# A limit of eight exponential tiles in flight in place of twelve, a ring of 13 tiles in place of 21, and spectral differences in tiles of their own

## The chip, the cores and the metric

The kernel runs on one core of one Trainium2 chip. The metric is the device time of one execution in microseconds (us); smaller is better. Engines: PE is TensorE (matrix products), ACT is ScalarE, DVE is VectorE, POOL is GpSimd, and SP starts most transfers. One launch computes the whole reference.

## What is computed

`x` is 2048 rows of 512 numbers. Two kinds of layers alternate, twice each: a filter in the two-dimensional spectrum, and attention with 32 query heads of 16 numbers that share one key head and one value head.

```python
def _A_ref(x, w_r, w_i):
    X = rfft2(x.astype(float32), axes=(-2, -1))
    y = irfft2(X * (w_r + 1j * w_i), s=(S, D), axes=(-2, -1)).astype(bfloat16)
    return y

def _B_ref(x, wq, wk, wv, wo):
    q = (x @ wq).reshape(B, S, 32, 16).transpose(0, 2, 1, 3)
    k, v = x @ wk, x @ wv
    scores = einsum("bhqd,bkd->bhqk", q, k) * 16 ** -0.5
    o = einsum("bhqk,bkd->bhqd", softmax(scores), v)
    return o.transpose(0, 2, 1, 3).reshape(B, S, 512) @ wo

x = x + _A_ref(_layernorm(x), w_r, w_i)
x = x + _B_ref(_layernorm(x), wq, wk, wv, wo)
x = x + _A_ref(_layernorm(x), w_r, w_i)
x = x + _B_ref(_layernorm(x), wq, wk, wv, wo)
```

Here `B` is 1, `S` is 2048, `D` is 512.

## The kernel before, in words

**A planner writes the order.** When the program is built, class `Plan` keeps a clock for each engine and, step by step, takes the piece of work that can start first by its own cost table (`MM` 220 ns for a round of products on PE, `ACT_EXP` 908 ns, `DVE_P1` 600 ns). Each choice emits the real instruction, through class `Emit`. Each engine then runs its instructions in the order in which they were emitted, and waits only on semaphores. What the planner counts, such as buffers in use, exists while the program is built; on the chip only the order and the waits are left.

**A pair of layers.** One `Layer` object is a spectral layer and the attention layer behind it; there are two. The spectral layer is a transform along each row on PE, a four-point step across the rows on DVE (`radix_g`), the middle of the transform on PE (`mid`), the product with the filter (`filt`), a step of sums and differences on DVE (`radix_d`, L58, "spectral differences" below), the inverse on PE (`inv`, L1211), a four-point step (`radix_v`, L66 to L76) and the last product back to rows. Then follow the normalization, K, V and the queries. Each layer's four groups `t` of rows deliver a part of K and V each, and attention begins with the first of them.

**Attention.** There are 32 blocks of four heads and 512 queries; a block has 16 chunks of 128 keys. A unit is one head, 512 queries, 128 keys. PE makes the scores of a unit with keys in one strip of 32 rows (`scores`, L1331). ACT takes units in pairs from the double buffers `sa` and writes the exponentials into a tile `e` (`exp`, L1336). DVE takes single units from the buffers `b`, with a first pass in whole numbers (`p1`, L1343) and two further phases that POOL mostly does (`phase`, L1347). PE then adds up V products, four heads at a time in four column strips (`pv`, L1353): one for each unit of ACT, three for each unit of DVE. Which engine takes which unit is decided by the planner as it goes (`peek`, `take`).

**The limit on tiles in flight.** `live["ACT"]` goes up when a pair's scores are emitted (`do_scores`) and down when the last V product that reads its tile is emitted (`do_pv`). `usable("ACT")` is false while `live["ACT"] >= bufs["ACT"]`, and then no scores for ACT may be emitted. `round` picks the heads of the next V round; it takes fewer than four heads only where the block has no more, where nothing else can go on, or where `full` holds, that is where `live` has reached `bufs` for ACT or for DVE:

```python
full = self.force or any(self.live[k] >= self.bufs[k] for k in ("ACT", "DVE"))
return sel if len(sel) == 4 or self.made(b0) or full else None
```

`bufs["ACT"]` is 8 (`E_BUFS`) from the middle of a layer's spectral part (`add_middle`) and 12 (`E_LATE`) from the moment its fourth V is complete (`v_got` in `add_back`).

**The ring of tiles.** `Emit.e2` holds 21 tiles of 1024 two-byte numbers in each partition. `t2` takes the one that has been free longest, `free2` puts one back at the end of the list. Who takes tiles: the exponentials, turned rows for the row transform (`tr_evac`, `turned`), `V` and the sums of `radix_v`, and the two halves of each spectral difference (`L.Dz`, two tiles for each of four groups `u`, each given back after its fourth reader in `inv`). Other tiles, of 2048 numbers, come from the pool `work` with tags (`t4`).

Of the kernel before, what the change touches and what calls it, by code (L numbers as in the profile page):

```python
# [8 lines left out]
ACT = mybir.ActivationFunctionType  # L9
# [43 lines left out]
    return tabs  # L53


def radix2(nc, o, x, piece):

    nc.vector.tensor_tensor(out=o, in0=x[:, 0:2, :], in1=x[:, 2:4, :], op=ALU.subtract if piece else ALU.add)  # L58


def radix4(nc, sd, x, half, o, piece):
# [53 lines left out]
class Plan:  # L115
# [12 lines left out]
    PORT = True  # L128
    POOL_LAG = 2600.0
    E_BUFS = 8  # L130
    E_LATE = 12
    T_BUFS = 4
    WIN = 3413.0
    WARM = 3500.0
# [552 lines left out]
class Layer:  # L687
# [83 lines left out]

    def add_middle(self):
        p, em = self.plan, self.em
        p.bufs["ACT"] = p.E_BUFS
        self.mid, self.fil = [], []
        for u in range(4):
            evs, two = [], u in self.two

            if two:
                outs = [((0, 2), (0, 1), 0), ((1, 3), (0, 1), 2)]  # L780
            else:
                outs = [((0, 1, 2, 3), (0, 1), 0), ((0, 1, 2, 3), (2, 3), 2)]
            if u % 2:
                outs = [(ts, (k,), o + i) for ts, ks, o in outs for i, k in enumerate(ks)]
            for ts, ks, o in outs:
                base, prev = None, []
                for t in ts:
                    deps, take = [self.g_done[t]] + prev, None
                    if not prev:
                        deps = deps + (self.gate if len(ks) == 2 else self.mm1_done[T - 1])  # L790
                        take = "sa" if len(ks) == 2 else "b"
                    k = p.add("PE", 434.0 * len(ks), deps, lambda k, u=u, ks=ks, t=t, ts=ts, base=base:
                              em.mid(self, u, ks, t, ts, (base or k).slot), take=take, order=10 + u)
                    base, prev = base or k, [k]
                evs.append(p.add("ACT", 909.0 if len(ks) == 2 else 482.0, prev, lambda k, u=u, o=o, n=len(ks), base=base:
                                 em.mid_evac(self, u, o, n, base.slot), give=(base,), order=10 + u))
            if two:
                evs = [self.pieces((600.0, 600.0), evs, lambda i, u=u: em.turn(self, u, i), 10 + u)]
            if u == 3 and not two:
                a = p.add("DVE", 1733.0, evs[:2], lambda k, u=u: em.filt(self, u, 0, 2), order=10 + u, port=True)  # L800
                mu = p.add("DVE", 1733.0, evs[2:] + [a], lambda k, u=u: em.filt(self, u, 2, 4), order=10 + u, port=True)
            else:
                mu = p.add("DVE", 3466.0, evs, lambda k, u=u: em.filt(self, u, 0, 4), order=10 + u, port=True)
            self.fil.append(mu)
            self.mid.append(self.pieces((600.0, 600.0), [mu], lambda i, u=u: em.radix_d(self, u, i), 26 if self.direct else 10 + u))
# [5 lines left out]
    def add_back(self):  # L811
        p, em, at = self.plan, self.em, self.at
        left = [T]
        for t in range(T):
# [53 lines left out]
            def v_got(k, t=t):  # L868
                at.v_ready[t] = k.end + p.LAT[k.eng]
                left[0] -= 1  # L870
                if left[0] == 0:
                    p.bufs["ACT"] = p.E_LATE
                if left[0] == self.EARLY:
                    at.dve_on = True
                    at.dve_from = k.end - 2000.0
# [61 lines left out]
class Emit:  # L937


    def __init__(self, ctx, tc, ins, out):  # L940
        nc = self.nc = tc.nc
        A_x, self.w_r, self.w_i, B_wq, B_wk, B_wv, B_wo = ins
        mk = lambda nm, b=1, **kw: ctx.enter_context(tc.tile_pool(name=nm, bufs=b, **kw))
        const = mk("const")
        psum = mk("psum", space=bass.MemoryType.PSUM)
        self.pool = mk("work")
        self.sa = [psum.tile([P, 2, 512], F32, name=f"sa{i}") for i in range(2)]
        self.b = [psum.tile([P, 512], F32, name=f"b{i}") for i in range(Plan.NB)]
        nc.scalar.preload_act_table_set("natural_log_exp_and_others")
        self.x = const.tile([P, R, T, 512], BF, name="x_sb")  # L950
        self.xv = A_x.flatten_outer_dims().rearrange("(r p t) d -> p r t d", r=R, p=P, t=T)
        ht = host_tables()
        self.dram = {k: nc.inline_tensor(v, name=f"const_{k}").ap() for k, v in ht.items()}
        tabs = {name: const.tile(list(ht[name].shape), BF, name=f"tab_{name}") for name in ("ident", "PH", "PS")}
        self.ident, self.PH, self.PS = tabs["ident"], tabs["PH"], tabs["PS"]
        nc.scalar.dma_start(out=self.ident, in_=self.dram["ident"])
        nc.scalar.dma_start(out=self.PH, in_=self.dram["PH"])
        self.way = mk("way", 2, space=bass.MemoryType.DRAM)
        self.wq = const.tile([P, NC, D], BF, name="wq")
        self.wk = const.tile([P, NC, DH], BF, name="wk")  # L960
        self.wk8 = const.tile([P, NC, P], BF, name="wk8")
        self.part = const.tile([P, 2], F32, name="part")
        self.wv = const.tile([P, NC, DH], BF, name="wv")
        self.tc = tc
        self.e2 = [const.tile([P, 1024], BF, name=f"e2_{i}") for i in range(21)]
        self.idle, self.home, self.writer = list(range(21)), {}, {}
        self.WO = const.tile([P, 4, D], BF, name="WO")
        self.junk = const.tile([P, 512], BF, name="junk")
        self.eps = const.tile([P, 1], F32, name="eps")
        self.zero = const.tile([P, 512], BF, name="zero")  # L970
        self.KA = const.tile([P, S], BF, name="KA")
        self.KB = const.tile([P, S], BF, name="KB")
        self.warm = const.tile([P, 2, 16], U16, name="warm")
        nc.vector.memset(self.zero, 0.0)
        nc.vector.memset(self.eps, EPS)
        nc.gpsimd.memset(self.warm, 0)
        self.key = const.tile([P, 1], F32, name="key")
        self.pw = phase_weights()
        self.VS = [const.tile([P, NT, 32], BF, name=f"vs{i}") for i in range(1 + K_PH)]
        for i, v in enumerate(self.VS):  # L980
            nc.gpsimd.memset(v, 1.0 if i == 0 else self.pw[i - 1])
        nc.gpsimd.int64_add(self.warm[:, 1].bitcast(U64), self.warm[:, 0].bitcast(U64), 0)
        half = (np.arange(P)[:, None] // DH % 2 == np.arange(2)).astype(np.float32)
        self.w_dma = [(self.PS, self.dram["PS"]), (self.wq, B_wq.rearrange("(c p) j -> p c j", p=P)),
                      (self.wk, B_wk.rearrange("(c p) j -> p c j", p=P)), (self.wv, B_wv.rearrange("(c p) j -> p c j", p=P)),
                      (self.part, nc.inline_tensor(half, name="const_part").ap()),
                      (self.WO, B_wo.rearrange("(g p) c -> p g c", p=P))]
        self.out_v = out.flatten_outer_dims().rearrange("(r p t) d -> p r t d", r=R, p=P, t=T)
# [178 lines left out]
    def turn(self, L, u, piece):  # L1167
        if piece == 0:
            L.sd_of[("x", u)] = self.t4([4, 512])
        radix2(self.nc, L.sd_of[("x", u)][:, 2 * piece:2 * piece + 2, :], L.X[u], piece)  # L1170
        if piece:
            L.X[u] = L.sd_of.pop(("x", u))

# [14 lines left out]

    def radix_d(self, L, u, piece):
        if piece == 0:  # L1190
            L.Dz[u] = [[self.t2([2, 512]), 4] for _ in range(2)]
            for z, _ in L.Dz[u]:
                self.writer.pop(self.home[id(z)][0], None)
        radix2(self.nc, L.Dz[u][piece][0], L.X[u], piece)

    def load_it(self, L, t):
        L.IT[t] = self.t4([4, 640], tag="it", bufs=2)
# [2 lines left out]
    def inv(self, L, t, b, j, slot, ks):  # L1200
        for v in range(T):
            if v <= t + 1 and v not in L.IT:
                self.load_it(L, v)
        ps = self.ps(slot).rearrange("p (u x) -> p u x", u=2)
        for k in ks:
            u = 2 * j + k
            for a in range(2):
                for i in range(2):
                    w = 128 * (3 - (t * a + i) % 4)
                    z = L.Dz[u][t % 2][0][:, a, 256 * i + 128 * b:256 * i + 128 * b + 128]  # L1210
                    self.nc.tensor.matmul(ps[:, k, :], lhsT=z, rhs=L.IT[t][:, u, w:w + 256], start=(a == 0 and i == 0),  # L1211
                                          stop=(a == 1 and i == 1), skip_group_check=True)
            d = L.Dz[u][t % 2]
            d[1] -= 1
            if d[1] == 0:
                self.free2(d[0])

    def inv0(self, L, b, j, slot, k):

# [255 lines left out]
```

## Time and profile before

| what | value |
| --- | --- |
| median of three runs | 1340.67 us (1340.6 to 1340.95) |
| the profiled execution | 1340.67 us |
| its span, first to last instruction | 1338.9 us |
| granted TensorE clock | 1.000 |
| attention of layer 1, first to last exponential | 73.9 to 674.3 us, 624 pairs on ACT, 800 units on DVE |
| attention of layer 2 | 736.1 to 1326.4 us, 619 pairs on ACT, 810 units on DVE |
| the wait of ACT for the scores of an exponential, longest two | 2.6 us, 2.2 us |

How to read what follows. The page gives each engine's busy time and its share of the span, then the span in 40 equal slices with the busy share in tenths; the row PEclk is the clock granted to TensorE in tenths. A stretch row begins with its limits in us and its length, then busy us and, in brackets, the number of instructions. A row of the timeline has start, duration, engine, line, operation and `out<-in`. A piece of the chain of waits has its start, its length, the engine, the tile, the line and the number of instructions. Several matmuls with the same start lie in different strips and run side by side; ends of matmuls are modelled, so their starts are read.

### The profile page before, as it was taken

To read this page: it belongs to the slowest core of one execution; us is meant where nothing else is said; L and a number is where in the kernel's file an instruction comes from. 1 tells how busy PE (TensorE), PEld (TensorE's weight loads), DVE (VectorE), ACT (ScalarE), POOL (GpSimd) and SP (SyncE) were. 2 spreads that over 40 slices of the span, in tenths; PEclk is the share of its full clock that TensorE was granted. 3 is DMA by queue.
4 is the path that set the end of the run, shared out by engine and by line. 5 is a ranking of instruction groups with operands and counts; after the bars stand their busy time and mean duration, and the time that the engine had idled before them with its cause. 6 is when DMAs were issued, how large, how long until landed. Compare 5 with 4: busy or idle time off the path is not lost.

```text
span 1338.9 us, 31412 instructions
## 1 busy us (share of the span) xinstructions
PE 1298.0 (97%) x12913; PEld 438.9 (33%) x12982; DVE 1281.7 (96%) x2297; ACT 1231.0 (92%) x1401; POOL 834.9 (62%) x819
## 2 busy tenths in 40 slices
PE   9999999999999999999999999999999999999998
PEld 4642223322232332222246422233222222232222
DVE  6998999999999999999979999999999999999998
ACT  6478999999999999999944899999999999999996
POOL 0004777766776678667720067787777767777775
PEclk9999999999999999999999999999999999999999
DMA  9100000010001000000051000000000000000000
GB/s 292 41 1 1 2 1 2 2 33 1 1 2 33 1 2 2 17 17 1 2 166 40 1 2 1 2 1 5 13 2 1 4 15 1 1 2 17 1 2 17
DMA packets 29040, 25.15 MB, mean 19 GB/s; under 512 B 8672, under 2 KB 27616, under 8 KB 28896
## 3 DMA queue, kind: packets, MB, share of 16 engines
q1 hardware_dynamic: 28608, 22.58, 5.6%
q8 instruction: 101, 1.65, 0.5%
q10 hardware_dynamic: 288, 0.56, 0.1%
q14 instruction: 43, 0.35, 0.1%
HBM read 17.89 MB, written 3.67 MB: 16 GB/s over the span
## 4 chain that ended last, share of the span: by engine, by line
ACT 48%; PE 30%; DVE 17%; issue 2%; DMA 1%; SPq 1%; POOL 0%; DVEq 0%; POOLq 0%
PE sa_64 L1331 3%; PE b_66 L1353 3%; PE b_69 L1353 3%; PE b_67 L1353 3%; ACT e_5_89 L1336 2%; ACT e_3_87 L1336 2%; ACT e_4_88 L1336 2%; ACT e_16_100 L1336 2%; PE sa_65 L1331 2%; ACT e_10_94 L1336 2%; ACT e_11_95 L1336 2%; ACT e_15_99 L1336 2%; ACT e_8_92 L1336 2%; ACT e_14_98 L1336 2%; ACT e_9_93 L1336 2%; ACT e_20_104 L1336 2%
## 5 line engine op out<-in xcount | busy, mean ns | idle before, releaser
L1331 PEld LDWEIGHTS <-KB 32*128 32x128 bf16 x2048 | 89.0, 91 | 229.0 <-issue 221.5
L1331 PEld LDWEIGHTS <-KA 32*128 32x128 bf16 x2048 | 83.4, 91 | 229.0 <-issue 219.4
L1353 PEld LDWEIGHTS <-vs_116 128*32 128x32 bf16 x2486 | 102.1, 94 | 97.6 <-issue 91.4
L1353 PEld LDWEIGHTS <-vs_117 128*32 128x32 bf16 x1610 | 97.1, 94 | 69.8 <-issue 68.1
L1353 PEld LDWEIGHTS <-vs_118 128*32 128x32 bf16 x1610 | 73.1, 94 | 75.7 <-issue 70.8
L1353 PEld LDWEIGHTS <-vs_119 128*32 128x32 bf16 x1610 | 71.9, 94 | 72.5 <-issue 67.9
L1347 POOL INT64_ADD w_1388<-w_1387 x1 | 1.0, 1039 | 110.7 <-DVE w_1387 L1343 110.7
L1347 POOL INT64_ADD w_10887<-w_10886 x1 | 1.0, 1037 | 98.5 <-DVE w_10886 L1343 98.5
L1040 DVE BATCH_NORM_STATS2 st<-x_sb 128x6 f32<-128x512 bf16 x52 | 35.4, 680 | 4.2 <-DMA x_sb<-in_A_x_dram 3.7
L1336 ACT ACTIVATE e_6_90<-sa_65 128x1024 bf16<-128x1024 f32 x32 | 35.4, 1107 | 1.3 <-PE sa_64 L1331 1.0
L1336 ACT ACTIVATE e_7_91<-sa_64 128x1024 bf16<-128x1024 f32 x33 | 36.2, 1097 | 0.3 <-PE sa_64 L1331 0.3
L1336 ACT ACTIVATE e_12_96<-sa_65 128x1024 bf16<-128x1024 f32 x32 | 35.5, 1110 | 0.9 <-PE b_68 L1331 0.8
L1336 ACT ACTIVATE e_14_98<-sa_65 128x1024 bf16<-128x1024 f32 x31 | 34.7, 1119 | 1.5 <-PE sa_64 L1331 1.4
L1336 ACT ACTIVATE e_13_97<-sa_65 128x1024 bf16<-128x1024 f32 x32 | 35.9, 1122 | 0.0
L1336 ACT ACTIVATE e_20_104<-sa_64 128x1024 bf16<-128x1024 f32 x32 | 35.9, 1121 | 0.0
L1336 ACT ACTIVATE e_8_92<-sa_65 128x1024 bf16<-128x1024 f32 x31 | 34.6, 1116 | 1.1 <-PE b_69 L1331 0.8
L1336 ACT ACTIVATE e_2_86<-sa_64 128x1024 bf16<-128x1024 f32 x32 | 35.3, 1103 | 0.0
L1336 ACT ACTIVATE e_17_101<-sa_65 128x1024 bf16<-128x1024 f32 x28 | 31.8, 1135 | 3.6 <-PE sa_64 L1331 3.6
L1336 ACT ACTIVATE e_4_88<-sa_64 128x1024 bf16<-128x1024 f32 x31 | 35.0, 1129 | 0.0
L1336 ACT ACTIVATE e_0_84<-sa_65 128x1024 bf16<-128x1024 f32 x30 | 33.5, 1117 | 1.3 <-PE sa_64 L1331 1.0
L1336 ACT ACTIVATE e_16_100<-sa_64 128x1024 bf16<-128x1024 f32 x31 | 34.6, 1118 | 0.0
L1336 ACT ACTIVATE e_17_101<-sa_64 128x1024 bf16<-128x1024 f32 x31 | 34.5, 1113 | 0.0
(4068 smaller groups left out, 6441.8 us busy)
## 6 DMA issues: line engine op xcount, KB each, us to landing
it<-const_IT SPq DMA_DIRECT2D x8, 640.0 KB, 6.3
x_sb<-in_A_x_dram SPq DMA_DIRECT2D x4, 512.0 KB, 6.9
out_dram<-x_sb SPq DMA_DIRECT2D x16, 128.0 KB, 1.8
way<-x_sb SPq DMA_DIRECT2D x6, 256.0 KB, 2.1
tab_PH<-const_PH ACTq DMA_DIRECT2D x1, 512.0 KB, 5.0
w_131<-const_FT SPq DMA_DIRECT2D x1, 512.0 KB, 8.8
w_136<-const_FT SPq DMA_DIRECT2D x1, 512.0 KB, 8.4
tab_PS<-const_PS SPq DMA_DIRECT2D x1, 512.0 KB, 7.8
```

The lines of the kernel that those rows point to most:

```text
L1040: self.nc.vector.bn_stats(st, self.ps(slot) if slot else self.x[:, x[1], x[0], :])
L1331: self.nc.tensor.matmul(o, lhsT=KX[rs, kc * P:(kc + 1) * P], rhs=at.QT[qb][rs, g, :], start=True, stop=True, skip_group_check=True)
L1336: self.wrote("ACT", e, self.nc.scalar.activation(out=e, in_=self.ps(slot), func=ACT.Exp, scale=SCALE))
L1347: self.nc.gpsimd.int64_add(t[p][:, 0:n].bitcast(U64), t[0][:, 0:n].bitcast(U64), DELTA[p] * FOUR)
L1353: self.nc.tensor.matmul(self.ps(slot)[32 * h:32 * h + 32, :], lhsT=V[:, kc, :], rhs=rhs, start=first, stop=last, skip_group_check=True)
```

## The change

The diff does three things.

1. The limit on ACT's pairs in flight stays at `E_BUFS`, 8; `E_LATE` is gone, in both layers.
2. The ring `e2` has 13 tiles in place of 21.
3. The spectral differences leave the ring. Each group `u` gets one tile of 2048 numbers under a tag of its own, `xd`, with four buffers; both halves lie in it. `inv` reads the same rows from there and gives nothing back. `radix2` takes the whole tile and the number of the half, and `turn` is written for that.

The diff comes with the words "Score heads of ScalarE's pairs and VectorE's tiles are chosen so that they lie in different 32-row strips of TensorE"; `peek`, which chooses the heads, is not in it.

```diff
-def radix2(nc, o, x, piece):
-
-    nc.vector.tensor_tensor(out=o, in0=x[:, 0:2, :], in1=x[:, 2:4, :], op=ALU.subtract if piece else ALU.add)
+def radix2(nc, sd, x, piece):
+
+    nc.vector.tensor_tensor(out=sd[:, 2 * piece:2 * piece + 2, :], in0=x[:, 0:2, :], in1=x[:, 2:4, :],
+                            op=ALU.subtract if piece else ALU.add)
...
     E_BUFS = 8
-    E_LATE = 12
...
     def add_middle(self):
         p, em = self.plan, self.em
-        p.bufs["ACT"] = p.E_BUFS
...
                 left[0] -= 1
-                if left[0] == 0:
-                    p.bufs["ACT"] = p.E_LATE
...
-        self.e2 = [const.tile([P, 1024], BF, name=f"e2_{i}") for i in range(21)]
-        self.idle, self.home, self.writer = list(range(21)), {}, {}
+        self.e2 = [const.tile([P, 1024], BF, name=f"e2_{i}") for i in range(13)]
+        self.idle, self.home, self.writer = list(range(13)), {}, {}
...
         if piece == 0:
             L.sd_of[("x", u)] = self.t4([4, 512])
-        radix2(self.nc, L.sd_of[("x", u)][:, 2 * piece:2 * piece + 2, :], L.X[u], piece)
+        radix2(self.nc, L.sd_of[("x", u)], L.X[u], piece)
...
         if piece == 0:
-            L.Dz[u] = [[self.t2([2, 512]), 4] for _ in range(2)]
-            for z, _ in L.Dz[u]:
-                self.writer.pop(self.home[id(z)][0], None)
-        radix2(self.nc, L.Dz[u][piece][0], L.X[u], piece)
+            L.Dz[u] = self.t4([4, 512], tag="xd", bufs=4)
+        radix2(self.nc, L.Dz[u], L.X[u], piece)
...
-                    z = L.Dz[u][t % 2][0][:, a, 256 * i + 128 * b:256 * i + 128 * b + 128]
+                    z = L.Dz[u][:, 2 * (t % 2) + a, 256 * i + 128 * b:256 * i + 128 * b + 128]
...
-            d = L.Dz[u][t % 2]
-            d[1] -= 1
-            if d[1] == 0:
-                self.free2(d[0])
```

## The prediction, made before the result was known

> **What bounds the kernel.** I read the busy row and the slices of the page first, then stretches of one engine at a time, then the chain of waits inside the worst stretch, then single tiles in the order of time.
>
> ```profile
> PE 1298.0 (97%) x12913; PEld 438.9 (33%) x12982; DVE 1281.7 (96%) x2297; ACT 1231.0 (92%) x1401; POOL 834.9 (62%) x819
> ...
> DVE  6998999999999999999979999999999999999998
> ACT  6478999999999999999944899999999999999996
> ...
> PEclk9999999999999999999999999999999999999999
> ```
>
> ScalarE (ACT) and VectorE (DVE) are full in slices 4 to 19 and 24 to 39: the two attention phases. The spectral phases lie in slices 1 to 3 and 20 to 23, where ACT has room. The clock is full throughout and is left out of what follows. What attention is worth per us comes from the stretches, taken for the exponentials (L1336, two units of 512 keys-by-queries each) and for VectorE's first pass (L1343, one unit each):
>
> ```profile
> core 0: us, ACT busy (x), PEclk, DMA share, GB/s
> 130.00:280.00 150.00, 149.80 (x164) 1.00 0.02 5
> 785.00:940.00 155.00, 154.84 (x170) 1.00 0.01 3
> ...
> 307.40:320.50 13.10, 12.08 (x13) 1.00 0.01 1
> 1074.40:1088.30 13.90, 13.68 (x16) 1.00 0.09 29
> ...
> core 0: us, DVE busy (x), PEclk, DMA share, GB/s
> 130.00:280.00 150.00, 133.90 (x220) 1.00 0.02 5
> 785.00:940.00 155.00, 141.13 (x232) 1.00 0.01 3
> ...
> 307.40:320.50 13.10, 7.09 (x13) 1.00 0.01 1
> 1074.40:1088.30 13.90, 8.81 (x16) 1.00 0.09 29
> ```
>
> Undisturbed attention does (2 x 164 + 220) / 150 = 3.65 units per us, and (2 x 170 + 232) / 155 = 3.69. I use 3.67. In the two short stretches it does (26 + 13) / 13.1 = 2.98 and (32 + 16) / 13.9 = 3.45: TensorE (PE) also has projection or query work there, and VectorE gets too few scores (13 first passes in 13.1 us, where 232 in 155 us would give 20). ACT keeps nearly its pace of 0.91 us a pair. So PE's order decides in the bursts, and ACT with DVE outside them.
>
> **Where the change can bite.** The limit on ACT's pairs in flight goes from 12 to 8 after the last V of a layer. A pair is in flight from its two sa matmuls on L1331 until the second of its two matmuls on L1353. Both stand in PE's own order, so the planner's count can be read off the trace: plus one at each pair's scores, minus one at the second reader.
>
> ```profile
> 400.26 1.24 ACT L1336 ACTIVATE e_18_102<-sa_64 128x1024 bf16<-128x1024 f32 x1
> ...
> 401.87 0.39 PE L1353 MATMUL b_67<-e_18_102,vs_116 128*32 128x512 bf16 x2
> ...
> 1076.76 1.18 ACT L1336 ACTIVATE e_19_103<-sa_65 128x1024 bf16<-128x1024 f32 x1
> ...
> 1087.08 0.39 PE L1353 MATMUL b_67<-e_19_103,vs_116 128*32 128x512 bf16 x2
> ```
>
> In plain attention a tile is read 1.6 us after its exponential began and the count is 2 to 4. In the burst the tile waits 10.3 us. Over the whole trace the count is above 8 for 31.0 us in seven places, with these peaks: 284 us (10), 307 to 320 (11), 574 (10), 942 (10), 1074 to 1093 (12), 1139 (9), 1227 (9). The sum of peaks less 8 is 2 + 3 + 2 + 2 + 4 + 1 + 1 = **15 pairs** that could no longer be put off. Pairs scored while the count stood above 8 number 42. Before 241.6 us the count does not reach 8 once the first V is complete, so until then PE's order should be that of before.
>
> **The limit, priced.** While the count stands at 8, PE may not score for ACT; `full` (in `round`) also lets it run a round of V products with fewer than four heads. It does V products, VectorE's scores or projections, then scores again. The pieces of the chain in the burst give the durations:
>
> ```profile
> 1079.30 0.32 PE sa_64 L1331 x2
> 1079.62 0.33 PE b_66 L1353 x4
> ...
> 1080.60 0.32 PE sa_65 L1331 x2
> 1080.93 0.55 PE b_66 L1353 x8
> ```
>
> Scoring a pair alone takes 0.32 us; a round of four V products takes 0.33, and a second round behind it 0.55 - 0.33 = 0.22. A pair needs half a round, 0.165 us. Putting off D pairs lets ACT run ahead by D half rounds. Without that, PE spends the same time on score and retirement together, so ACT loses D x 0.165 / (0.32 + 0.165) = 0.34 D pairs. For D = 15 that is 5.1 pairs, 10.2 units, and 10.2 / 3.67 = **2.8 us**. Ends: if every one of the 15 is lost to ACT, 30 / 3.67 = **8.2 us**. If ACT's other score buffer always covers the delay (it has about 0.91 - 0.32 = 0.6 us to hide one round) the loss is 0. I take 2.8, since both engines are full on either side of a burst and PE is nearly always busy within it. Queued behind a late pair on ACT are the flexible copies of queries and, in layer 2's front, the scalings on L1124; VectorE's radix steps wait for those.
>
> The Trainium skill, "TensorEngine Tiling (Array Packing)", section Key Properties, says that changing the tiling mode drains TensorE. It speaks against a lower limit, because fewer pairs ahead mean more changes between score strips and V columns. The trace agrees with a cost: 0.32 to 0.33 us for a first round against 0.22 for one in the same mode. Charging two such changes of 0.10 us to each of the 42 pairs would give 42 x 2 x 0.10 = 8.4 us in place of 2.8. I do not follow it, because score and V runs already alternate in the burst, so most of these changes are paid before.
>
> **Tiles, 21 to 13.** Exponentials, transposed rows, `V` and its radix sums share the ring. Taking the tiles' first writes and last reads, without the spectral differences at most 11 are held at once in the two ramps (70 to 90 and 740 to 750 us), so two of 13 are free. A tile can then be handed out again soon after its last reader is issued, where before at least eight were free. The wait is at most what is left of that reader: 0 to 0.33 us of a V round or 0.42 us of a radix step, perhaps a handful of times. ACT is busy 28.73 of 40 us from 60 to 100, which covers it; without that cover six such waits would be 6 x 0.4 = 2.4 us. In the bursts eight pairs, at least one of them not yet written, and two transposed tiles leave four free. I take **0.3 us**, and 0 to 2.4 for the range.
>
> **Spectral differences in their own four tiles.** L58 keeps 16 instructions of 0.68 us on VectorE for the same data; the four L.Dz tiles are first needed again a layer later (L58 at 43 to 55 us, then from 706), long after their readers. No DMA, no queue and no instruction is added: 0. Eight ring tiles of 2 KB go and four of 4 KB come, so memory is equal. Each half still holds the same two rows, and the planner orders the readers after both halves already. If a reader had to wait for the second half it would be one 0.68 us step a tile, hidden because PE has the other groups' work; uncovered, 4 x 0.68 = 2.7 us a layer. I take 0.
>
> **Sum.** 1340.67 + 2.8 + 0.3 + 0 = 1343.8; call it **1343.8 us**. The profiled execution took 1340.67 us too (span 1338.9 and 1.8 around it), equal to the median of the three runs, so nothing has to be carried over. The planner is greedy, and after the first refusal its order differs everywhere. The tails show what that is worth: ACT stands idle 5.3 us at the end of layer 1's attention and 10.8 at the end of layer 2's, and another order can shift each by some 2 us. So the forecast's own range is 1341 to 1348.
>
> **Rivals.**
> (a) *The limit is hidden.* Peaks are brief: five of the seven places are at or below 10, and one round (0.33 us) fits the 0.6 us that ACT's other buffer gives. Against: 1074 to 1088, where the count stays high for 11 us. Loss 0.5 us or less: **1341.0**.
> (b) *Faster: VectorE gets what ACT gives up.* In the eight stretches that make up the bursts (41.5 us) DVE is idle 41.5 - 35.1 = 6.4 us and ACT 0.6. At 0.6 us a first pass that is 10.7 units. If PE, forbidden to feed ACT, feeds VectorE sooner, and ACT loses nothing through its second buffer, the gain is 10.7 / 3.67 = 2.9 us: **1337.8**. It decides once VectorE regains more units than ACT loses, above 10.2. Against: VectorE's scores need a free bank, and projections and the V sums hold those in a burst.
> (c) *The full price.* Each put-off pair is lost whole, as with the 8.2 us above, or rounds of two or three heads waste PE: **1348.9**. For: PE has no idle time in the bursts. Against: there are other pairs' V products to choose from.
> (d) *The change does not do what its words say.* They speak of score heads in different strips, but `peek`, which picks them, is not in the diff. I expect score groups as before and give this no time of its own.
>
> **How the numbers follow.** What a measurement of this kernel can tell from no change is about 0.2%, 2.7 us: 1338.0 to 1343.35. Forecast 0.56 (of it 0.42 above that band, 0.12 in it, 0.02 below); (a) 0.12, in it; (b) 0.16, below it; (c) 0.16, above. Slower 0.42 + 0.16 = 0.58; same 0.12 + 0.12 = 0.24; faster 0.02 + 0.16 = 0.18. For 8 in 10 the range goes from 1338 to 1350, with half of (b) and the upper half of (c) outside.
>
> **What would show it.** Right: a count that never passes 8 after the V's, gaps of 0.3 to 1 us on ACT before exponentials with PE as the releaser near projections, 5 pairs' worth in all, and undisturbed stretches still at 3.65 to 3.69 units per us. Wrong: DVE's idle time in the bursts gone without such gaps (b); unchanged bursts (a); waits of exponentials on L1353 or L75 (the ring costs more); a different pace outside the bursts, or tails that move by more than 3 us, which would make the order after the first refusal the main cause.

## The result, and the profile after

The changed kernel takes 1346.59 us (median of four runs, 1346.21 to 1348.28) against 1340.81 us for the kernel before. The ratio is 1.0046 with a 95% interval of 1.0028 to 1.0063: slower by 5.8 us. The profiled execution took 1346.21 us, its span is 1344.3 us, 5.4 more than before. These rows of the page answer to those shown of before:

```profile
PE 1303.0 (97%) x12950; PEld 442.1 (33%) x13017; DVE 1291.4 (96%) x2313; ACT 1224.3 (91%) x1393; POOL 843.7 (63%) x827
...
DVE  6998999999999999999979999999999999999998
ACT  6478999999998999999954889999899998999996
...
PEclk9999999999999999999999999999999999999999
```

ACT is idle 1344.3 - 1224.3 = 120.0 us where it was 107.9, with slices of 8 inside attention that were 9. DVE is idle 52.9 us where it was 57.2. By the count of exponentials and first passes, eight pairs, 16 units, went from ACT to DVE: 1235 pairs and 1626 units, before 1243 and 1610. The attention of layer 1 carries most of the loss: its last exponential begins 4.4 us later than before, layer 2's first one 4.0 us later and its last 5.4 us later.

Undisturbed attention kept its pace. Here are the two stretches of before (the second moved by 4 us), exponentials first and VectorE's first passes second:

```profile
core 0: us, ACT busy (x), PEclk, DMA share, GB/s
130.00:280.00 150.00, 149.80 (x163) 1.00 0.02 5
789.00:944.00 155.00, 154.94 (x170) 1.00 0.01 3
...
core 0: us, DVE busy (x), PEclk, DMA share, GB/s
130.00:280.00 150.00, 133.41 (x219) 1.00 0.02 5
789.00:944.00 155.00, 141.42 (x232) 1.00 0.01 3
```

(2 x 163 + 219) / 150 = 3.63 and (2 x 170 + 232) / 155 = 3.69 units per us, against 3.65 and 3.69. The loss lies in a few places. This is the worst, in the order of time on the changed kernel:

```profile
427.02 0.39 PE L1322 MATMUL sa_64<-w_4725,KA 32*128 32x512 bf16 x2
427.03 0.38 PE L1322 MATMUL b_66<-w_4725,KA 32*128 32x512 bf16 x1
...
427.43 1.02 PE L1375 MATMUL b_68<-WO,w_3956 128*128 128x512 bf16 x4
...
429.22 1.02 PE L1108 MATMUL b_66<-tab_PH,e_1_85 128*128 128x512 bf16 x4 [0.23 <-DVE w_6084 L1334]
...
431.02 0.59 PE L1019 MATMUL b_67<-zero 128*128 128x512 bf16 x2 [0.23 <-DVE w_6084 L1334]
...
431.45 1.02 PE L1108 MATMUL b_67<-tab_PH,e_1_85 128*128 128x512 bf16 x4
...
432.40 0.39 PE L1344 MATMUL b_68<-e_0_84,vs_108 128*32 128x512 bf16 x2
...
433.17 1.02 ACT L1327 ACTIVATE e_2_86<-sa_65 128x1024 bf16<-128x1024 f32 x1 [4.42 <-PE sa_65 L1322]
```

At 427.02 the eighth pair is scored. No V product (L1344) follows for 5.4 us, so no tile comes free. PE makes scores for VectorE, projections (L1375), a row transform (L1108) and even two idle products on zeros (L1019), which the planner puts in where PE's recent work is below its threshold. Projections, row transforms and query products are called background pieces below: the planner keeps them in a list of their own, beside scores and V rounds. The first V round at 432.40 lifts the refusal, and ACT has waited 4.42 us. A second place of the same kind, where PE runs three background pieces in a row (two projections and a query product, L1306):

```profile
1225.20 1.04 PE L1375 MATMUL b_66<-WO,w_15758 128*128 128x512 bf16 x4
...
1226.08 1.03 PE L1375 MATMUL b_68<-WO,w_15758 128*128 128x512 bf16 x4
...
1226.94 1.03 PE L1306 MATMUL b_69<-gx,wq 128*128 128x512 bf16 x4
...
1227.90 0.39 PE L1344 MATMUL b_67<-w_17474,vs_111 128*32 128x512 bf16 x2
...
1229.31 1.02 ACT L1327 ACTIVATE e_8_92<-sa_65 128x1024 bf16<-128x1024 f32 x1 [2.93 <-PE sa_64 L1322]
```

Counted as in the prediction, the pairs in flight never pass 8 after the V's and reach 8 at 57 places in attention. Of the 23.4 us that ACT is idle in attention (ramps and ends of the layers left out), 18.6 lie at such a place or within 1 us behind it. The second longest stall of all is of another kind: ACT waits 3.54 us at 1117.2 us while the count stands at 4 or less and V rounds run, because the next scores need new queries (products L1306, cast on L1266). Before has such waits too, 2.56 us at 457.9 us and 1.35 us at 1114.2 us.

### The profile page after: what moved, and what is told of

Same layout as the page of the kernel before. It is cut to its first block, busy times and chain, and to the rows that moved or that the text cites. A ratio compares the mean times of both kernels' runs of the same rounds, so it can differ in the third digit from the quotient of the medians.

```text
span 1344.3 us, 31506 instructions
## 1 busy us (share of the span) xinstructions
PE 1303.0 (97%) x12950; PEld 442.1 (33%) x13017; DVE 1291.4 (96%) x2313; ACT 1224.3 (91%) x1393; POOL 843.7 (63%) x827
## 3 DMA queue, kind: packets, MB, share of 16 engines
HBM read 17.89 MB, written 3.67 MB: 16 GB/s over the span
## 4 chain that ended last, share of the span: by engine, by line
ACT 60%; PE 22%; DVE 16%; issue 2%; DVEq 0%; ACTq 0%
ACT e_11_95 L1327 5%; ACT e_0_84 L1327 5%; ACT e_1_85 L1327 5%; ACT e_8_92 L1327 5%; ACT e_6_90 L1327 5%; ACT e_2_86 L1327 5%; ACT e_4_88 L1327 4%; ACT e_10_94 L1327 4%; ACT e_7_91 L1327 4%; ACT e_3_87 L1327 4%; ACT e_12_96 L1327 4%; ACT e_9_93 L1327 4%; ACT e_5_89 L1327 4%; PE b_67 L1344 2%; PE sa_65 L1322 2%
## 5 line engine op out<-in xcount | busy, mean ns | idle before, releaser
L1344 PEld LDWEIGHTS <-vs_108 128*32 128x32 bf16 x2470 | 102.4, 93 | 97.7 <-issue 90.3
L1344 PEld LDWEIGHTS <-vs_109 128*32 128x32 bf16 x1626 | 97.1, 94 | 70.5 <-issue 69.0
L1344 PEld LDWEIGHTS <-vs_111 128*32 128x32 bf16 x1626 | 74.0, 94 | 79.0 <-issue 74.7
L1344 PEld LDWEIGHTS <-vs_110 128*32 128x32 bf16 x1626 | 71.6, 94 | 75.0 <-issue 70.6
L1327 ACT ACTIVATE e_8_92<-sa_65 128x1024 bf16<-128x1024 f32 x49 | 55.0, 1122 | 4.1 <-PE sa_64 L1322 4.1
L1327 ACT ACTIVATE e_6_90<-sa_65 128x1024 bf16<-128x1024 f32 x50 | 55.7, 1115 | 2.7 <-PE sa_64 L1322 2.5
L1327 ACT ACTIVATE e_7_91<-sa_65 128x1024 bf16<-128x1024 f32 x49 | 55.0, 1121 | 1.2 <-PE sa_64 L1322 1.0
L1327 ACT ACTIVATE e_12_96<-sa_65 128x1024 bf16<-128x1024 f32 x49 | 54.8, 1119 | 1.3 <-PE sa_64 L1322 0.9
L1327 ACT ACTIVATE e_11_95<-sa_64 128x1024 bf16<-128x1024 f32 x50 | 55.9, 1118 | 0.1
L1327 ACT ACTIVATE e_2_86<-sa_65 128x1024 bf16<-128x1024 f32 x46 | 51.8, 1127 | 4.4 <-PE sa_65 L1322 4.4
L1327 ACT ACTIVATE e_9_93<-sa_64 128x1024 bf16<-128x1024 f32 x49 | 54.8, 1118 | 0.8 <-PE b_69 L1322 0.8
L1327 ACT ACTIVATE e_4_88<-sa_65 128x1024 bf16<-128x1024 f32 x46 | 51.5, 1120 | 4.4 <-PE sa_64 L1322 3.5
L1327 ACT ACTIVATE e_3_87<-sa_65 128x1024 bf16<-128x1024 f32 x48 | 53.9, 1124 | 1.5 <-PE b_68 L1322 0.7
L1327 ACT ACTIVATE e_5_89<-sa_64 128x1024 bf16<-128x1024 f32 x49 | 55.0, 1121 | 0.1
L1327 ACT ACTIVATE e_5_89<-sa_65 128x1024 bf16<-128x1024 f32 x47 | 53.2, 1132 | 1.7 <-PE sa_64 L1322 1.4
L1327 ACT ACTIVATE e_2_86<-sa_64 128x1024 bf16<-128x1024 f32 x48 | 54.3, 1131 | 0.1
L1327 ACT ACTIVATE e_10_94<-sa_65 128x1024 bf16<-128x1024 f32 x48 | 54.1, 1128 | 0.0
L1327 ACT ACTIVATE e_0_84<-sa_65 128x1024 bf16<-128x1024 f32 x48 | 53.9, 1123 | 0.1
```

The source lines that it names most:

```text
L1327: self.wrote("ACT", e, self.nc.scalar.activation(out=e, in_=self.ps(slot), func=ACT.Exp, scale=SCALE))
L1344: self.nc.tensor.matmul(self.ps(slot)[32 * h:32 * h + 32, :], lhsT=V[:, kc, :], rhs=rhs, start=first, stop=last, skip_group_check=True)
```

## The experiments

Times are medians. "Before" was timed again on the same chip with each group: 1340.73 to 1340.84 us. Ratios are to it, with their 95% intervals.

**The limit alone, and everything but the limit.** On the kernel before:

```diff
-    E_LATE = 12
+    E_LATE = 8
```

> Before with E_LATE 8 and nothing else: ring of 21, spectral differences in the ring. Theory (the limit): the whole 5.8 us comes from scores that PE may no longer make for ACT, so 1346.6 us (1345.5 to 1347.5), ACT with some 8 pairs fewer and DVE with 16 units more than before. Rival (the ring of 13 or the differences' own tiles): 1340.8 us, as before.

Measured: 1346.58 us, ratio 1.0044 (1.0028 to 1.0061), 1235 pairs and 1626 units. On the changed kernel, the other way round:

```diff
     E_BUFS = 8
+    E_LATE = 12
...
+        p.bufs["ACT"] = p.E_BUFS
         self.mid, self.fil = [], []
...
                 left[0] -= 1
+                if left[0] == 0:
+                    p.bufs["ACT"] = p.E_LATE
```

> The changed kernel with the limit put back to 12 after the last V of a layer; ring of 13 and the differences' own tiles stay. Theory (the limit): 1340.8 us, up to 1342 if tiles handed out early make exponentials wait in the bursts. Rival (the ring): 1345 us or more, with waits of exponentials on V products.

Measured: 1340.67 us, ratio 1.0004 (0.9995 to 1.0013), with a ring of 13 and a limit of 12. So the limit is the change of time, and ring and differences' tiles together cost nothing that these times can tell: 1346.58 and 1346.59 us with limit 8, 1340.67 and 1340.81 with limit 12. On ACT, POOL and PE the first kernel runs the changed kernel's sequence of instructions, and the second runs that of before. What ACT waited for ahead of its exponentials, first with the limit of 8 and then with 12:

```profile
L1336 ACT ACTIVATE e<-sa x1235: 1005/1117/1352, 74.1 to 1332.3; 128x1024 bf16<-128x1024 f32 x177
...
  PE sa L1331: 21.0, 18
  PE b L1331: 5.4, 10
```

```profile
L1331 ACT ACTIVATE e<-sa x1243: 1005/1114/1352, 74.0 to 1327.7; 128x1024 bf16<-128x1024 f32 x178
...
  PE sa L1326: 11.2, 13
  PE b L1326: 3.6, 8
```

The last two rows of each give us and times for the scores that were late. 26.4 us against 14.8 (13.8 in the profile of before): the limit makes ACT wait 11.6 us more, for scores and not for V products that would still read a tile.

**Other limits.** The same line of before with 10, and with 16.

> Before with E_LATE 10. Theory (the limit): only two bursts go above 10, by 1 and by 2 pairs of the 15, so 3/15 of 5.8 us: 1342.0 us. Rival (the order after the first refusal is another draw of a greedy planner, and its scatter makes the difference): anywhere from 1337 to 1348, with no relation to 10 lying between 8 and 12.

> Before with E_LATE 16. Theory (the limit): the count of before touches 12 for 2.0 us in one burst, so at most one or two refusals go away: 1340.0 to 1340.8 us. Rival (scatter of the greedy order after 1076 us): 1337 to 1345.

Measured: 1338.06 us, ratio 0.9971 (0.9961 to 0.9980), for 10; 1338.71 us, ratio 0.9983 (0.9974 to 0.9993), for 16. Neither theory's number came, and both rivals' ranges were met: 10 is faster than 12, and 16 faster by 2.1 us although its sequence on PE first differs at 1080 us. The time does not fall evenly from 8 to 16. Past 8, other orders scatter by 2 to 3 us, even one that differs so late.

**Is 8 slow, or was its order a bad draw?** The planner's cost table was moved by a trifle, which gives other greedy orders, each with both limits.

```diff
-    PE_SW = 102.0
+    PE_SW = 104.0
```

> Limit 8 alone, and the planner's cost of a change of mode PE_SW is 104 ns in place of 102, which shifts its greedy order and says nothing new of the chip. Theory (8 is slow in itself): 1344.5 to 1348 us. Rival (8 drew a bad order): anywhere from 1338 to 1348, as likely near 1340 as near 1346.

> Before with PE_SW 104 ns in the planner in place of 102. Theory (the limit costs more than the order scatters): 1337.5 to 1342 us, below the 1346.1 us of limit 8 with the same 104. Rival (12 is no better, it drew a good order): 1343 to 1348.

```diff
-    ACT_EXP = 908.0
+    ACT_EXP = 910.0
```

> Limit 8 alone with ACT_EXP 910 ns in the planner in place of 908. Theory (8 is slow in itself): 1344 to 1348 us. Rival (scatter): as likely near 1340.

> Before with ACT_EXP 910 ns in place of 908. Theory: 1337.5 to 1342 us, and 3 to 8 us below limit 8 with the same 910. Rival (scatter): within 2 us of limit 8 with 910, on either side.

| planner's table | limit 8 | limit 12 | difference | pairs on ACT, 8 and 12 |
| --- | --- | --- | --- | --- |
| as it was | 1346.58 us | 1340.81 us | 5.8 us | 1235, 1243 |
| PE_SW 104 | 1346.09 us | 1340.83 us | 5.3 us | 1236, 1246 |
| ACT_EXP 910 | 1342.06 us | 1335.56 us | 6.5 us | 1235, 1247 |

Against before the four are 1.0038 (1.0025 to 1.0052), 0.9999 (0.9989 to 1.0010), 1.0009 (0.9999 to 1.0020) and 0.9959 (0.9943 to 0.9975), in the order of the expectations. Two absolute expectations were missed (with 910 both limits came 1.9 us below their ranges), because that table moves limit 8 by 4.5 us and limit 12 by 5.2. But 8 costs 5.3 to 6.5 us against 12 in each of three orders. As far as three orders tell, the rival of a bad draw falls for 8 against 12; it stands for 10, 12 and 16 among each other. The last kernel of the table beats both kernels of this study. Since both limits gain from 910, this can be the luck of another order or the table itself; no run separates the two.

**What holds the V rounds back while ACT is refused.** On the kernel with limit 8, a V round is taken ahead of its turn while the limit holds:

```diff
-                c.append((t_pv, 1, self.do_pv, sel))
+                c.append((t_pv - (500.0 if self.live["ACT"] >= self.bufs["ACT"] else 0.0), 1, self.do_pv, sel))
```

> Limit 8 alone (1346.6 us), and while the count stands at the limit a V round is taken 500 ns ahead of its turn, before projections and query products. Theory (while ACT is refused, PE runs whole 0.87 us background pieces instead of the V rounds that would lift the refusal, as at 1225 to 1228 us of the changed kernel): ACT's waits of 2 us and more near projections shrink, 1342.5 to 1344.5 us. Rival (bank shortage is what holds the V rounds): 1346 us. Rival (scatter of the greedy order): anything from 1338 to 1348.

Or the last free PSUM bank is kept for the block whose V products are due. A bank is one of the four buffers `b` into which PE writes; scores for VectorE, background pieces and the sums of V products share them.

```diff
+    def keep(self):
+
+        if self.live["ACT"] < self.bufs["ACT"] or not self.pv:
+            return 0
+        return 0 if min(e[2] for e in self.pv) in self.acc_of else 1
...
+            free = max(0, free - self.keep())
             if not free or sd >= 3 or ...
...
             if k.take and not k.step:
+                if k.take == "b" and sum(x is None for x in self.use) <= self.keep():
+                    continue
```

> Limit 8 alone, and while the count stands at the limit and the oldest block with V products due has no PSUM bank, the last free bank is kept for it (VectorE's scores and PE's background work may not take it). Theory (the 4.4 us stall at 428.6 us of the changed kernel comes from V products that had no bank): that stall and others after a block's end go, 1342 to 1344.5 us. Rival (no bank shortage elsewhere): 1345.5 us or more. Rival (scatter): anything from 1338 to 1348.

And both:

> Limit 8 with V rounds first and the bank kept. Theory (both stalls together are the cost): 1339 to 1342 us, with no wait of an exponential over 2 us but the two at block changes that the kernel before has as well. Rival (PE time is what the limit costs, as forecast): at least 1343.5 us.

Measured: V first 1339.1 us, ratio 0.9984 (0.9975 to 0.9993); the bank kept 1346.7 us, ratio 1.0041 (1.0027 to 1.0055); both 1340.69 us, ratio 0.9998 (0.9988 to 1.0007). Keeping a bank leaves the sequences on ACT, DVE and POOL as they were, PE's up to 1092 us, and the 4.42 us stall too. No choice at that stall hung on the last free bank, so a lack of banks falls as its cause.

With V first, the waits ahead of exponentials fall from 26.4 to 17.2 us. Neither of the two stalls shown above is left; the longest waits in attention are now 3.00 us at 604.1 us, where ACT waits for new queries (L1315, cast on L1275), and 1.53 us at 1084.8 us. The time falls by 7.5 us, more than the limit had cost. That is below the theory's range, and of the expectations only the rival of scatter allowed it. "Both" came out in its theory's range, but not as the theory said: a wait of 4.38 us stands at 604.1 us, again for new queries, where before's longest are 2.56 and 2.22 us, and the kernel is 1.6 us slower than with V first alone.

So V first gains something besides, and its control is the same line with limit 12:

> Before (limit 12) with the V round 500 ns ahead of its turn while the count stands at the limit in force, which is 8 in the ramps. Theory (V first repairs what the refusal at 8 costs, and 12 is hardly refused): 1339.5 to 1341.5 us. Rival (V first gains in the ramps, or wherever it stands): 1333 to 1338 us, that is before less the 7.5 us that it gained at 8.

Measured: 1336.64 us, ratio 0.9971 (0.9959 to 0.9984). The theory's range was missed and the rival's met: V first gains 4.1 us at 12 as well. Its order differs from 82 us on, in the ramp (the first us of a layer's attention, while its K and V are still being made), where the limit is 8 in every kernel. With V first, 8 costs 1339.1 - 1336.64 = 2.5 us against 12, where it cost 5.3 to 6.5 without. This is one pair of orders, and the two intervals overlap. ACT still gives up seven pairs and waits 17.2 - 9.6 = 7.6 us more with the limit of 8 (first) than with 12:

```profile
L1336 ACT ACTIVATE e<-sa x1242: 1004/1112/1352, 74.0 to 1324.7; 128x1024 bf16<-128x1024 f32 x178
...
  PE sa L1331: 12.9, 15
  PE b L1331: 4.3, 7
```

```profile
L1336 ACT ACTIVATE e<-sa x1249: 1004/1125/1352, 73.7 to 1322.1; 128x1024 bf16<-128x1024 f32 x179
...
  PE sa L1331: 6.6, 8
  PE b L1331: 3.0, 6
```

## Why the prediction was right, point by point

**Direction and range held; the size of the limit's term was half of what was measured.** The sum gave 1343.8 us, and 1346.59 was measured, within the forecast's own 1341 to 1348.

- *The limit.* Priced at 2.8 us, measured 5.8 (1346.58 against 1340.81). The step that failed is that PE, refused for ACT, "does V products, VectorE's scores or projections, then scores again", so that ACT loses a third of each pair put off. In the stalls shown the planner took background pieces and VectorE's scores ahead of the V rounds that would have lifted the refusal. The forecast's sign was gaps of 0.3 to 1 us, 5 pairs' worth; the two stalls are 4.42 and 2.93 us, and ACT's extra wait of 11.6 us is 11.6 / 0.91 = 12.7 pairs' worth, near the ceiling of 15 and not the 5.1 of the sum. With V rounds put first, which is what the price assumed, 8 against 12 measured 2.5 us. That is near the 2.8, but part of this can be luck: it is one pair of orders, orders scatter by as much, and ACT's extra wait was still 7.6 us, 8.4 pairs' worth. So the stalls show the step that failed; how much of the missing 3 us it accounts for is not shown.
- *What it is worth (an estimate).* 12.7 pairs are 25.4 units, 25.4 / 3.67 = 6.9 us. DVE's idle time fell by 4.3 us, 7.2 units at 0.6 us, worth 2.0. The rest, 4.9 us, is close to the 5.4 by which the span grew. So rival (b), VectorE taking what ACT gives up, is there, at less than a third of what ACT loses.
- *The places.* The forecast's bursts were those of before, with most of the weight at 1074 to 1093 us. Up to 283 us the order on PE was the same, as forecast. After that the bursts moved: the largest stall, at 428.6 us, lies where before had no count above 8. A trace of before did not give the places.
- *The ring of 13, 0.3 us.* Measured 0: the medians with and without it differ by 0.15 us or less at both limits.
- *The differences' own tiles, 0.* Measured together with the ring: 0.
- *The rivals.* (a), that the limit is hidden, is refuted by the intervals. (c), the full price of 8.2 us, comes close in pairs (12.7 of 15), not in time, since (b) gives some back. Rounds of fewer heads did not become common: groups of four V products number 1804 after and 1794 before. (d): score groups of four, three, two and one numbered 195, 735, 428 and 255 before, and 203, 730, 407 and 280 after, so heads are picked much as before.
- *The tails.* From the end of layer 2's last exponential to the end of the span ACT is idle 11.3 us in both kernels; the gap behind layer 1's attention is 5.3 us before and 4.8 after. The order after the first refusal does scatter, by up to 5 us between planner tables; the three orders with limit 8, 1342.06 to 1346.58 us, all lie in the forecast's range.

The Trainium skill, "TensorEngine Tiling (Array Packing)", section Key Properties, says that a change of tiling mode drains TensorE. Charged to each pair with the 0.10 us of the forecast's rows, that rival stood at 8.4 us. The measured 5.8 came by another way: in the order in which PE ran them, score strips, V columns and full products change 2472 times in the trace of before and 2478 times after, and by estimate that is 6 x 0.10 = 0.6 us.

What stays open is how much of V first's gain comes from the ramps and how much from the refusals in attention; no run separates them, and only one pair of orders was run with it. Why 10 and 16 beat 12 stays open too.

## What to carry to other kernels

A limit on buffers in flight is not priced by how far the peaks go above it alone. Ask which work frees a buffer, and whether the scheduler puts that work first once the limit is reached; here the same limit cost 5.3 to 6.5 us with background work ahead and, in the one pair of orders that was run, 2.5 us with the freeing work first. Where a greedy planner writes the order, compare a parameter over several orders (a cost moved by 2 ns will do) before a few us are called its effect.

## What the runs showed that was not expected

A change of 2 ns in the planner's table, 908 to 910 for an exponential, took 5.2 us off the kernel before (1335.56 us), nearly as much as the change of this study added. The ring of tiles could shrink from 21 to 13 with twelve pairs allowed in flight and cost nothing (1340.67 us).
